# Nystromformer attention and a multiplicative FFN on one core: v pieces gated later, q landmarks' block form on GpSimd, the last chunk on two engines and two queues

## The chip, the cores and the metric

The kernel runs on one core of one Trainium2 chip. The time is device microseconds of one execution. A kernel's time is the median of its runs. A profile is one execution recorded by the hardware profiler; its span goes from the first to the last instruction, and times inside a trace count from the span's start.

## The reference

Attention by landmarks for 8 batches and 8 heads, 576 rows of 64, then a feed-forward network on all 4608 rows:

```python
q_lm = q.reshape(B, H, 32, 18, D).mean(axis=3)      # 32 landmarks, each the mean of 18 rows
k_lm = k.reshape(B, H, 32, 18, D).mean(axis=3)
A  = softmax(q    @ k_lm.T / 8)                     # 576 x 32
Bm = softmax(q_lm @ k_lm.T / 8)                     # 32 x 32
C  = softmax(q_lm @ k.T    / 8)                     # 32 x 576
Z  = Bm.T / (norm1(Bm) * norminf(Bm) + 1e-6)
for _ in range(6):
    Z = 2 * Z - Z @ Bm @ Z
x = (A @ Z @ C @ v)                                 # heads side by side: 4608 x 512
out = ((x @ w1) * (x @ w2)) @ w3 @ w_out            # widths 512, 1024, 1024, 512
```

All inputs and the output are float32.

## The kernel before

**Start and fold.** The kernel first multiplies w3 and w_out into one matrix `w34` (`fold`, lines 472 to 516; its matmuls are L497, its transposes L484), while q, k and v of the first batches arrive. The attention of batch 0 is woven into that by hand (lines 598 to 611).

**The loop over batches.** `for b in range(B)` (lines 616 to 643) has two halves. In the up half, for each of eight column groups j, `up(st, j, 0)` and `up(st, j, 1)` multiply batch b by the two up weights (L439, PSUM tiles `big`). ScalarE copies the first product to `a_sb` (L443), VectorE multiplies it with the second into `ab` (L445). In the down half `down` multiplies 128 rows at a time by `w34`, in two halves of four matmuls (L457); after the second half ScalarE copies the sums to `o_sb` (L461) and SyncE stores them (L467). An even batch has four such chunks, an odd one five; the last batch's fifth ends the program.

**What runs beside it.** Between these steps the loop advances a generator, `attention(sts[b + 1])`, by `steps(at)`: five steps in the up half, one behind it, the rest in the down half. Its first step (lines 199 to 213) adds the two landmark parts on TensorE (L201), copies them to fp16 `lm` on ScalarE (L206), and builds `qbd` (L208): the q landmarks laid out in blocks, where each pair of heads has its landmarks in the upper or the lower 64 partitions and zeros elsewhere, by a product with the 0/1 column pair `par`. The second step makes the 32 x 32 scores (L217, L221) and their softmax on VectorE (L224 to L230). The third and fourth make the scores of C (`scores_c`, L242, which read `qbd`), their exponentials `ect` (L246) and partial sums on GpSimd (L253 to L258). The fifth multiplies them with v (`cv`, L323 and L328). Six inversion steps (L382) and the product with the up weights (L425) follow.

**Loads.** For batch b + 2 the loop sends four DMA transposes of q and k on SyncE at the start of block b (`turn_all`, L106), four pieces of v in its up half (`load_v_piece`, L84 and L85), and at j = 5 the landmark sums on GpSimd (`landmarks`, L183 to L192), among which GpSimd issues the q and k loads of batch b + 3 (`qk_pieces`, L93). A v piece is 288 KB, two heads. ScalarE writes one column of its tile first (L84), and the DMA on SyncE waits for that write, so the place of the copy in ScalarE's queue holds the load back. In the version before, the copy reads `a_sb`, at j = 4, 5, 6 and 7.

**What sets the order.** Each engine runs its instructions in program order, which is written out by hand (`manual_schedule`). PSUM has three `big` tiles of two banks, one `small` and one `acc`; a tile is written again when its last reader is done, and which one a product gets is decided when the kernel is built. SyncE's queue holds transposes, v pieces and stores, GpSimd's holds its sums and the q and k loads.

Of the kernel before, what the change touches and what calls it, by code (L numbers as in the profile page):

```python
# [9 lines left out]
AXF = mybir.ActivationFunctionType  # L10
ALU = mybir.AluOpType
AX = mybir.AxisListType

B = 8
H = 8
S = 576
# [4 lines left out]
DM = 512  # L21
# [3 lines left out]
X64 = 64.0  # L25
NP = 96
# [5 lines left out]
def kernel(  # L32
# [11 lines left out]
    nc = tc.nc  # L44
# [8 lines left out]
    def big():  # L53
        return psp.tile([128, 2, 512], FP32, name="big", bufs=3)
# [25 lines left out]
    def load_v_piece(st, b, i, done):  # L80
        if i == 0:
            st["vt"] = pin.tile([128, H, 384], FP32, name="vt")
        hs = slice(2 * i, 2 * i + 2)
        nc.scalar.copy(out=st["vt"][0:NP, 2 * i, 0:1], in_=done)  # L84
        nc.sync.dma_start(out=st["vt"][0:NP, hs],  # L85
                          in_=v[b, hs].rearrange("h (p r) d -> p h (r d)", p=NP))

    def qk_pieces(st, b):
        st["qkn"] = pin.tile([128, 2, H, 384], FP16, name="qkn")
        for t, src in ((1, k), (0, q)):  # L90
            for i in range(2):
                hs = slice(4 * i, 4 * i + 4)
                nc.gpsimd.dma_start(out=st["qkn"][0:NP, t, hs, :],  # L93
                                    in_=src[b, hs].rearrange("h (p r) d -> p h (r d)", p=NP))
                yield
# [29 lines left out]
    ident = consts.tile([128, 128], FP32, name="ident")  # L125
# [49 lines left out]
    def landmarks(st, t, eng=nc.gpsimd, pieces=iter(())):  # L175
        if "parts" not in st:
            st["parts"] = pz.tile([128, 2, 2, H, 32], FP16, name="parts")
        for h0 in ((0,) if eng is nc.gpsimd else (0, 4)):
            own, n = ("", H) if eng is nc.gpsimd else ("v", 4)
            hs = slice(h0, h0 + n)  # L180
            x = st["qkT"][:, t, hs, :, :]
            tr = pat.tile([128, n, NP], FP32, name="tr" + own, bufs=1)
            eng.tensor_tensor(out=tr, in0=x[:, :, 0, :], in1=x[:, :, 1, :], op=ALU.add)  # L183
            eng.tensor_tensor(out=tr, in0=tr, in1=x[:, :, 2, :], op=ALU.add)  # L184
            next(pieces, None)
            t3 = tr.rearrange("p h (l g) -> p h l g", g=3)
            o = pat.tile([128, n, 32], FP32, name="o3" + own, bufs=1)
            hi, lo = st["parts"][:, 0, t, hs, :], st["parts"][:, 1, t, hs, :]
            eng.tensor_tensor(out=o, in0=t3[:, :, :, 0], in1=t3[:, :, :, 1], op=ALU.add)
            eng.tensor_tensor(out=o, in0=o, in1=t3[:, :, :, 2], op=ALU.add)  # L190
            eng.tensor_copy(out=hi, in_=o)
            eng.tensor_tensor(out=lo, in0=o, in1=hi, op=ALU.subtract)  # L192
            next(pieces, None)


    def attention(st, bank=None):
# [3 lines left out]
        for i in range(2):  # L200
# [4 lines left out]
        lm = pat.tile([128, 2, H, 32], FP16, name="lm")  # L205
        nc.scalar.copy(out=lm, in_=pl)  # L206
        qbd = pat.tile([128, H, 2, 32], FP16, name="qbd")
        nc.vector.tensor_tensor(  # L208
            out=qbd,
            in0=lm[:, 0, :, :].unsqueeze(2).to_broadcast([128, H, 2, 32]),  # L210
            in1=par.unsqueeze(1).unsqueeze(3).to_broadcast([128, H, 2, 32]),
# [3 lines left out]
        for qd in range(2):  # L215
            for h in range(4):
# [5 lines left out]
                             func=AXF.Exp, scale=SCALE / (GRP * GRP))  # L222
# [27 lines left out]
        def presum(qd):  # L250
# [21 lines left out]
                                scalar1=-1.0, scalar2=-1e-6, op0=ALU.mult, op1=ALU.add)  # L272
# [8 lines left out]
            out=bmbd, in0=bmn.unsqueeze(2).to_broadcast([128, 2, 4, 32]),  # L281
# [29 lines left out]
        for qd in range(2):  # L311
            nc.vector.tensor_scalar(out=sz_[:, qd, 0:32], in0=psR[:, 32 * qd:32 * qd + 32],
                                    scalar1=nrn[:, qd:qd + 1], scalar2=None, op0=ALU.mult)
            nc.vector.scalar_tensor_tensor(
                out=tz_[:, qd, :], in0=psR[:, 32 * qd:32 * qd + 32], scalar=nrn[:, qd:qd + 1],
# [58 lines left out]
        for it in range(6):  # L374
            last = it == 5
            psI = big()
            o = 32 if last else 0
# [25 lines left out]
        for qd in range(2):  # L403
# [7 lines left out]
                                       op0=ALU.mult, op1=ALU.subtract)  # L411
# [5 lines left out]
        for n in range(2):  # L417
            for w in range(2):
# [11 lines left out]
                else:  # L430
                    nc.vector.tensor_scalar(out=g[:, :, w, fs], in0=psG, scalar1=1.0 / ZS,  # L431
                                            scalar2=None, op0=ALU.mult)
            yield

    def up(st, j, w):
        p = big()
        for qd in range(2):
            for c in range(2):
                nc.tensor.matmul(p[:, c, 0:HS], st["g"][:, qd, w, 128 * j:128 * j + 128],  # L439
                                 st["ahat"][qd][:, c, :], start=(qd == 0), stop=(qd == 1))  # L440
        if w == 0:
            st["a_sb"] = po.tile([128, 2, HS], FP16, name="a_sb", bufs=2)
            nc.scalar.copy(out=st["a_sb"], in_=p[:, :, 0:HS])  # L443
        else:
            nc.vector.tensor_tensor(  # L445
                out=st["ab"][:, j, st["t0"]:st["t0"] + S].rearrange("p (c s) -> p c s", c=2),
                in0=st["a_sb"], in1=p[:, :, 0:HS], op=ALU.mult)


    rows = out.rearrange("(b p g) f -> b g p f", b=B, g=6)  # L450

    def down(ab, b0, t0, half, hold, bank):
        if half == 0:
            hold["ps"] = bank()
        pso = hold["ps"]
        for j in range(4 * half, 4 * half + 4):
            nc.tensor.matmul(pso[:, :], ab[:, j, t0:t0 + 128], w34[:, j, :],  # L457
                             start=(j == 0), stop=(j == 7))
        if half == 1:
            o_sb = po.tile([128, DM], FP32, name="o_sb")  # L460
            nc.scalar.activation(out=o_sb, in_=pso[:, :], func=AXF.Copy,  # L461
                                 scale=1.0 / (X64 * X64))
            o = 0
            while o < 128:
                gi, p0 = divmod((t0 + o) % S, NP)
                n = min(128 - o, NP - p0)
                nc.sync.dma_start(out=rows[b0 + (t0 + o) // S, 2 * (gi % 3) + gi // 3, p0:p0 + n, :],  # L467
                                  in_=o_sb[o:o + n, :])
                o += n


# [46 lines left out]
    sts = [dict() for _ in range(B)]  # L518

    def turn_all(b):  # L520
        for t in (1, 0):
            for h0 in (0, 4):
                transposes(sts[b], t, range(h0, h0 + 4))

    def steps(g, n=1):
        for _ in range(n):
            next(g, None)
# [3 lines left out]
    with tc.tile_pool(name="pf", bufs=2) as pf:  # L531
# [64 lines left out]
        turn_all(1)  # L596
        steps(fd, 6)
        at = attention(sts[0])
        for n, m in enumerate((2, 2, 2, 3, 3, 2, 1, 1, 1, 1, 2, 2, 3, 3)):
            steps(at)  # L600
# [10 lines left out]
        steps(fd, 64)  # L611
    pab = ctx.enter_context(tc.tile_pool(name="pab", bufs=2))
    at = attention(sts[1], acc)


    for b in range(B):
        st = sts[b]
        if b % 2 == 0:
            ab = pab.tile([128, 8, 2 * S], FP16, name="ab")
        st["ab"], st["t0"] = ab, S * (b % 2)  # L620
        if b + 2 < B:
            turn_all(b + 2)
        chunks = range(0, 512, 128) if b % 2 == 0 else range(512, 2 * S, 128)
        for j in range(8):
            up(st, j, 0)
            steps(at, (1, 1, 1, 0, 1, 0, 1, 0)[j])
            if b + 2 < B and j > 3:
                load_v_piece(sts[b + 2], b + 2, j - 4, st["a_sb"][0:NP, 0, 0:1])
            up(st, j, 1)
            if b + 2 < B and j == 5:  # L630
                pieces = qk_pieces(sts[b + 3], b + 3) if b + 3 < B else iter(())
                landmarks(sts[b + 2], 1, pieces=pieces)
                landmarks(sts[b + 2], 0, pieces=pieces)
        steps(at, 1)
        nxt = attention(sts[b + 2], acc) if b + 2 < B else iter(())
        hold = {}
        nd = 2 * len(chunks)
        for n in range(nd):
            bank = (lambda: big()[:, 0, :]) if n // 2 % 2 else acc
            down(ab, b - b % 2, chunks[n // 2], n % 2, hold, bank)  # L640
            steps(at)
        steps(at, 30)
        at = nxt
# [30 lines left out]
```

## Time and profile before

| | us |
|---|---|
| median of 4 runs | 289.15 |
| the runs | 285.31, 287.9, 290.39, 294.48 |
| profiled execution | 285.31 |
| its span | 283.5 |

The profile is of the fastest of these runs; about 1.8 us of its time lie around the span. TensorE is busy for 270.5 us of the span (95%), VectorE for 165.7, GpSimd for 153.2 and ScalarE for 130.2. In the page a group's row gives the line, the engine, the operation, output and input tiles with their shapes and the count, then busy time, the mean duration of one in ns, and the idle time of the engine just before these instructions with what ended it. The chain of work is followed back from the last instruction to what released each step; "issue" in it is time in which the engine waited for nothing that the profile shows. PEld is the weight load of TensorE, SPq and ACTq are the queues from which SyncE and ScalarE issue DMAs. The DMA engines are busy for nine tenths of most slices until 225 us and for less after that.

### The profile page before, as it was taken

How to read it: one execution, taken by the hardware profiler on the slowest of the kernel's cores; microseconds unless marked ns; L12 is line 12 of the kernel's file. 1: busy time of each engine (PE TensorE's matmuls, PEld its weight loads, DVE VectorE, ACT ScalarE, POOL GpSimd, SP SyncE). 2: the span in 40 equal slices, each digit the busy share in tenths (PEclk: the TensorE clock that was granted, in tenths of full speed). 3: DMA queues.
4: the chain of work that ended last, by engine and by line, in shares of the span. 5: the costliest groups of instructions: out<-in, count | busy, mean ns of one | idle time of the engine just before them, and what ended most of it. 6: DMA issues, size and time to landing. Idle time of an engine off the chain costs nothing.

```text
span 283.5 us, 9486 instructions
## 1 busy us (share of the span) xinstructions
PE 270.5 (95%) x3996; PEld 152.3 (54%) x3996; DVE 165.7 (58%) x430; ACT 130.2 (46%) x235; POOL 153.2 (54%) x202
## 2 busy tenths in 40 slices
PE   7999899999999997999999999998999999999993
PEld 3466455444674475347645754574458446834741
DVE  7743144653577575746766775576577756675620
ACT  2643254223661664157527732672276245625531
POOL 1617824595179739942895499259917950500000
PEclk9999999999999999999999999999999999999999
DMA  6999999999946999997898989997899622013024
GB/s 207 312 242 260 233 248 159 199 238 121 146 124 129 185 164 183 180 172 150 193 161 164 171 208 181 178 169 182 146 180 161 186 79 76 5 37 91 24 71 114
DMA packets 61978, 45.57 MB, mean 161 GB/s; under 512 B 35568, under 2 KB 54000, under 8 KB 61936
## 3 DMA queue, kind: packets, MB, share of 16 engines
q1 hardware_dynamic: 47392, 32.12, 49.5%
q0 software_dynamic: 13824, 11.54, 30.2%
q10 hardware_dynamic: 720, 1.31, 1.4%
q8 instruction: 31, 0.51, 0.8%
q14 instruction: 11, 0.09, 0.1%
HBM read 38.80 MB, written 9.44 MB: 170 GB/s over the span
## 4 chain that ended last, share of the span: by engine, by line
PE 83%; ACT 5%; POOL 4%; issue 3%; DVE 2%; DMA 1%; ACTq 0%; DVEq 0%; POOLq 0%
PE big L439 22%; PE acc L457 13%; PE big L457 11%; PE acc L497 10%; PE big L382 6%; PE big L425 5%; ACT a_sb L443 3%; PE small L323 2%; PE big L367 2%; PE acc L323 2%; PE big L484 2%; PE big L242 2%; DMA w3f<-in_moe_w_dram 1%; PE small L497 1%; PE big L292 1%
## 5 line engine op out<-in xcount | busy, mean ns | idle before, releaser
L439 PE MATMUL big<-ahat,gt 128*128 128x288 f16 x512 | 73.3, 286 | 2.0 <-ACT a_sb L443 1.6
L439 PEld LDWEIGHTS <-gt 128*128 128x128 f16 x512 | 48.4, 98 | 21.4 <-issue 7.4
L445 DVE TENSOR_TENSOR ab<-a_sb,big 128x576 f16<-128x576 f16 x64 | 48.0, 749 | 14.6 <-ACT a_sb L443 10.8
L443 ACT CAST a_sb<-big 128x576 f16<-128x576 f32 x64 | 40.9, 639 | 32.2 <-PE big L439 31.1
L253 POOL TENSOR_TENSOR t<-ect 96x384 f32<-96x384 f32 x16 | 15.9, 994 | 62.4 <-ACT ect L246 53.8
L497 PE MATMUL acc<-wsp,w3t 128*128 128x512 f16 x168 | 40.6, 379 | 0.7 <-ACT w L500 0.5
L457 PE MATMUL acc<-w,ab 128*128 128x512 f16 x160 | 40.3, 381 | 0.0
L457 PEld LDWEIGHTS <-ab 128*128 128x128 f16 x288 | 24.0, 98 | 29.0 <-issue 4.2
L457 PE MATMUL big<-w,ab 128*128 128x512 f16 x128 | 32.7, 381 | 0.0
L461 ACT ACTIVATE o_sb<-acc 128x512 f32<-128x512 f32 x20 | 11.9, 597 | 42.0 <-PE acc L457 42.0
L183 POOL TENSOR_TENSOR tr<-qkT 128x768 f32<-128x768 f16 x16 | 26.3, 1642 | 7.3 <-DMA qkT<-qkn 7.3
L497 PEld LDWEIGHTS <-w3t 128*128 128x128 f16 x192 | 18.1, 98 | 20.6 <-issue 1.8
L431 DVE TENSOR_SCALAR gt<-big 128x1024 f16<-128x1024 f32 x16 | 19.6, 1225 | 15.3 <-PE big L425 15.3
L184 POOL TENSOR_TENSOR tr<-tr,qkT 128x768 f32<-128x768 f32 x16 | 26.3, 1641 | 1.3
L429 ACT ACTIVATE gt<-big 128x1024 f16<-128x1024 f32 x16 | 16.4, 1024 | 11.9 <-PE big L425 11.9
L490 DVE SCALAR_TENSOR_TENSOR w3t<-big,w3t 128x512 f16<-128x512 f32 x16 | 11.0, 690 | 14.0 <-ACT w3t L489 14.0
L461 ACT ACTIVATE o_sb<-big 128x512 f32<-128x512 f32 x16 | 9.6, 597 | 19.0 <-PE big L457 19.0
L425 PE MATMUL big<-wup,zt 64*32 64x512 f16 x512 | 17.4, 380 | 0.7 <-issue 0.7
L489 ACT ACTIVATE w3t<-big 128x512 f16<-128x512 f32 x16 | 9.5, 594 | 12.4 <-PE big L484 12.3
L208 DVE TENSOR_TENSOR qbd<-lm,par 128x512 f16<-128x512 f16 x8 | 5.5, 692 | 15.8 <-ACT lm L206 15.8
L246 ACT ACTIVATE ect<-big 96x768 f32<-96x768 f32 x16 | 12.9, 807 | 3.6 <-PE big L242 2.9
L190 POOL TENSOR_TENSOR o<-o,tr 128x256 f32<-128x256 f32 x16 | 12.9, 806 | 1.3
(317 smaller groups left out, 373.1 us busy)
## 6 DMA issues: line engine op xcount, KB each, us to landing
vt<-in_v_dram SPq DMA_DIRECT2D x28, 288.0 KB, 4.5
out_dram<-o_sb SPq DMA_DIRECT2D x24, 192.0 KB, 3.2
qkn<-in_k_dram POOLq DMA_DIRECT2D x12, 288.0 KB, 5.3
qkn<-in_q_dram POOLq DMA_DIRECT2D x12, 288.0 KB, 5.5
w3f<-in_moe_w_dram SPq DMA_DIRECT2D x6, 512.0 KB, 7.0
out_dram<-o_sb SPq DMA_DIRECT2D x24, 128.0 KB, 3.4
wup<-in_moe_w_dram POOLq DMA_DIRECT2D x4, 512.0 KB, 32.2
out_dram<-o_sb SPq DMA_DIRECT2D x24, 64.0 KB, 2.9
```

What stands on the lines that cost most here:

```text
L183: eng.tensor_tensor(out=tr, in0=x[:, :, 0, :], in1=x[:, :, 1, :], op=ALU.add)
L184: eng.tensor_tensor(out=tr, in0=tr, in1=x[:, :, 2, :], op=ALU.add)
L382: nc.tensor.matmul(psI[32 * t:32 * t + 32, qd, o:96], tz_[sl, qd, :], sz_[sl, qd, o:96], start=True, stop=True, tile_position=(32 * h, 32 ...
L425: nc.tensor.matmul(psG[32 * h:32 * h + 32, qd, :], zt[rs, i, h, :], wup[rs, h, w, fs], start=(i == 0), stop=(i == 1), tile_position=(64 * ...
L429: nc.scalar.activation(out=g[:, :, w, fs], in_=psG, func=AXF.Copy, scale=1.0 / ZS)
L431: nc.vector.tensor_scalar(out=g[:, :, w, fs], in0=psG, scalar1=1.0 / ZS, scalar2=None, op0=ALU.mult)
L439: nc.tensor.matmul(p[:, c, 0:HS], st["g"][:, qd, w, 128 * j:128 * j + 128], st["ahat"][qd][:, c, :], start=(qd == 0), stop=(qd == 1))
L443: nc.scalar.copy(out=st["a_sb"], in_=p[:, :, 0:HS])
L445: nc.vector.tensor_tensor(out=st["ab"][:, j, st["t0"]:st["t0"] + S].rearrange("p (c s) -> p c s", c=2), in0=st["a_sb"], in1=p[:, :, 0:HS], ...
L457: nc.tensor.matmul(pso[:, :], ab[:, j, t0:t0 + 128], w34[:, j, :], start=(j == 0), stop=(j == 7))
L461: nc.scalar.activation(out=o_sb, in_=pso[:, :], func=AXF.Copy, scale=1.0 / (X64 * X64))
L497: nc.tensor.matmul(psW[j][:, :], turned[j, c // 4][:, a, c % 4, :], wsp[:, b, c, :], start=(c == 0 and a + b == 0), stop=(c == 7 and a == 1))
```

## The change

Three edits. The product that forms `qbd` is issued on GpSimd instead of VectorE. The four v pieces of batch b + 2 are issued at j = 6 and 7 and behind the first and the second finished chunk of the down half, and the column written ahead of each comes from the constant `ident` instead of `a_sb`. For the last chunk of the last batch (`final`), VectorE copies columns 256 to 511 and ScalarE columns 0 to 255 of the sums, and the second of its two stores (96 rows; the first has 32) goes out on ScalarE's DMA queue.

```diff
@@ -205,7 +205,7 @@ attention
         nc.scalar.copy(out=lm, in_=pl)
         qbd = pat.tile([128, H, 2, 32], FP16, name="qbd")
-        nc.vector.tensor_tensor(
+        nc.gpsimd.tensor_tensor(
             out=qbd,
             in0=lm[:, 0, :, :].unsqueeze(2).to_broadcast([128, H, 2, 32]),
             in1=par.unsqueeze(1).unsqueeze(3).to_broadcast([128, H, 2, 32]),
@@ -458,14 +458,20 @@ down
             o_sb = po.tile([128, DM], FP32, name="o_sb")
-            nc.scalar.activation(out=o_sb, in_=pso[:, :], func=AXF.Copy,
+            final = b0 == B - 2 and t0 == 2 * S - 128
+            if final:
+                nc.vector.tensor_scalar(out=o_sb[:, 256:DM], in0=pso[:, 256:DM],
+                                        scalar1=1.0 / (X64 * X64), scalar2=None, op0=ALU.mult)
+            c = slice(0, 256 if final else DM)
+            nc.scalar.activation(out=o_sb[:, c], in_=pso[:, c], func=AXF.Copy,
                                  scale=1.0 / (X64 * X64))
             o = 0
             while o < 128:
                 gi, p0 = divmod((t0 + o) % S, NP)
                 n = min(128 - o, NP - p0)
-                nc.sync.dma_start(out=rows[b0 + (t0 + o) // S, 2 * (gi % 3) + gi // 3, p0:p0 + n, :],
-                                  in_=o_sb[o:o + n, :])
+                eng = nc.scalar if final and o else nc.sync
+                eng.dma_start(out=rows[b0 + (t0 + o) // S, 2 * (gi % 3) + gi // 3, p0:p0 + n, :],
+                              in_=o_sb[o:o + n, :])
                 o += n
@@ -624,8 +630,8 @@ the loop over batches
         for j in range(8):
             up(st, j, 0)
             steps(at, (1, 1, 1, 0, 1, 0, 1, 0)[j])
-            if b + 2 < B and j > 3:
-                load_v_piece(sts[b + 2], b + 2, j - 4, st["a_sb"][0:NP, 0, 0:1])
+            if b + 2 < B and j > 5:
+                load_v_piece(sts[b + 2], b + 2, j - 6, ident[0:NP, 0:1])
             up(st, j, 1)
@@ -638,6 +644,8 @@
             down(ab, b - b % 2, chunks[n // 2], n % 2, hold, bank)
+            if b + 2 < B and n in (1, 3):
+                load_v_piece(sts[b + 2], b + 2, 2 + n // 2, ident[0:NP, 0:1])
             steps(at)
```

## The prediction

> **What bounds the kernel now.** I read the page first (engines, slices, chain by engine), then the chain of work in order of time for one block of the steady loop, then the timeline of that block by engine, then the waits and the tail. The page's engine line and its chain line say the same thing:
>
> ```profile
> PE 270.5 (95%) x3996; PEld 152.3 (54%) x3996; DVE 165.7 (58%) x430; ACT 130.2 (46%) x235; POOL 153.2 (54%) x202
> PE 83%; ACT 5%; POOL 4%; issue 3%; DVE 2%; DMA 1%; ACTq 0%; DVEq 0%; POOLq 0%
> ```
>
> TensorE sets the time; whatever the other engines do counts only where TensorE stands still for it. The granted clock is 0.998, so no clock effect is in these numbers. The batch blocks start (first L439 matmul) at 71.7, 97.55, 126.89, 153.03, 180.69, 207.67, 235.33 and 261.29. In a block the chain is matmul after matmul with one short break, at its start (block 3):
>
> ```profile
> 155.26 1.24 PE big L439 x8
> 156.50 0.03 ACTq L443
> 156.53 0.04 issue
> 156.57 0.65 ACT a_sb L443
> 157.21 0.04 issue
> 157.25 2.26 PE big L439 x16
> ```
>
> The page's "issue" share has a second break, in block 1 only, in the middle of a run of small matmuls:
>
> ```profile
> 109.10 0.04 PE acc L328 x5
> 109.14 1.50 issue
> 110.64 0.20 PE acc L328 x2
> ```
>
> and its table of DMA queues has the likely reason, TensorE's program arriving in 31 pieces of 16 KB:
>
> ```profile
> q8 instruction: 31, 0.51, 0.8%
> ```
>
> One piece starts at 108.09 and takes 1.10 us; matmuls resume 1.45 us after it. Block 4 has the same picture: a piece from 192.34 to 193.43, TensorE idle until 194.92, 1.49 us after it. The waits name DVE ab L445 for that (1.3 us at the longest, where the other six blocks have about 0.25), but the same instruction in block 3 started 0.06 us after the ab it needs. So 1.5 + 1.0 = 2.5 us are lost to late program pieces in the blocks.
>
> **qbd on GpSimd.** Per batch one VectorE instruction goes and one GpSimd instruction comes. The timeline of block 3:
>
> ```profile
> 154.27 0.59 ACT L206 CAST lm<-small 128x512 f16<-128x512 f32 x1
> 154.89 0.69 DVE L208 TENSOR_TENSOR qbd<-lm,par 128x512 f16<-128x512 f16 x1 [0.50 <-ACT lm L206]
> 155.50 0.75 DVE L445 TENSOR_TENSOR ab<-a_sb,big 128x576 f16<-128x576 f16 x1
> 156.32 0.69 PE L242 MATMUL big<-qbd,qkT 128*96 128x64 f16 x12
> 157.99 0.99 POOL L253 TENSOR_TENSOR t<-ect 96x384 f32<-96x384 f32 x1 [4.98 <-ACT ect L246]
> ```
>
> GpSimd is idle from 153.0 to 157.99, so it can start when lm is done, at 154.93. Its duration is not in the trace; the nearest row is the other product of broadcasts, L280:
>
> ```profile
> L280 POOL TENSOR_TENSOR bmbd<-bmn,mask 128x256 f32<-128x256 f32 x8 | 5.8, 730 | 0.6
> ```
>
> Against L277 (64 elements, 290 ns) that is 440/192 = 2.3 ns an element, so 512 elements take 730 + 256 x 2.3 = 1.32 us. The low end is the slope from L253 (384, 994) to L183 (768, 1642): 1.21; the high end is L190's 806/256 = 3.15 ns: 1.61. I take 1.32: qbd is ready at 156.25, where TensorE reaches L242 at 156.32. Nothing is lost. There is more cover: after L242's 12 matmuls (0.53 us of issue) TensorE waits for a_sb until 157.25 anyway, so qbd may come as late as 156.72, a duration of 1.73 us.
>
> What VectorE gains: the first ab no longer queues behind qbd. It needs the matmuls that end at 154.62, so it runs 154.7 to 155.45 instead of to 156.25. The L224 to L230 chain then waits only for ebm (155.91), 0.22 earlier, and so does the second ab (ends 157.6, not 157.82). The L439 group that takes the bank of this second ab started at 157.88, 0.63 after its forerunner at 157.25, where a free-running group takes 0.49; 0.13 us go. The stall before 157.25 stays: its a_sb waits for TensorE itself. So 7 x -0.13 = **-0.9 us** (if a different PSUM bank is handed out, the 0.15 before 155.84 may go as well: -2.0; with 1.73 us passed by 0.3: +2). In the fold, qbd ends at 37.3 where L242 starts at 38.87: nothing.
>
> The Trainium skill speaks against this edit: GPSIMD Engine Reference, "Engine selection", sends two-input elementwise work to VectorE, about 2x faster. Its factor of 1.96 on the 692 ns of L208 is 1.36 us, by which the edit would cost 8 x 0.67 = +5.4 us if it lay on the path. The row it has to be read with is L253's idle time, 4.98 us here and 53.8 in the page: the engine is empty there, and the sum by the trace is 0 or below. I go by the trace.
>
> **v pieces later.** In blocks 0 to 5 the four gates (0.19 us on ACT) and DMAs (288 KB on SP) move from j = 4, 5, 6, 7 to j = 6, 7 and to the first and second finished chunk. In block 3 the issues were at 162.0, 162.6, 164.2, 166.6; they become 164.2, 166.6, about 170.9 and 173.2 (each behind two stores of its chunk). The first was already late, as SP was sending transposes until 161.86. No gate waits for anything: the constant is always there and the vt buffer was read a block ago. On ACT two gates leave a stretch where it waits for TensorE anyway, and the new ones stand behind an o_sb copy, where ACT idles 2.0 to 2.5 us: zero. On SP, behind the last piece come stores (175.1) and, at 182.5, the next transposes: free. v is used in the next block, at 190.7, 17 us after its issue, for a landing of 4.5: hidden. In the DMA engines 576 KB now run beside the q and k pieces of GpSimd; at the 300 GB/s of the page's busiest slices (312 at most) that is an estimated 1.9 us. The last q piece (issued 152.32 in block 2, 5.5 to landing) would land at 159.7 instead of 157.8; the transpose that reads it goes out at 160.0, and GpSimd reads the result at 171.7. Hidden, with 7 us in reserve.
>
> What it can bring is the program pieces. In block 1 v issues at 107.1 and 108.6, just when the piece of 108.09 is wanted, and in block 4 at 189.4 and 190.3, before the one of 192.34. The Trainium skill, Runtime: NRT & Kernel Launch, "Instruction fetch mechanics", calls crossing a 16 KB boundary mostly hidden, because instructions go out slower than they arrive: by that rule this part is worth 0. The trace has 1.5 and 1.0 us, where TensorE runs through 256 instructions in 2.1 us (106.9 to 109.0). The transposes stay in the way, so I take a third of 2.5 us off, -0.8. Against it stands block 2: its piece landed at 140.08 and was needed at 141.82, 0.3 us more than the 1.45; a v piece now comes at 138. I put +0.4 on that. Sum **-0.4 us** (ends -2.5 and +1.5).
>
> **Last chunk.** Now:
>
> ```profile
> 277.23 1.74 PE acc L457 x8
> 279.04 0.60 ACT o_sb L461
> 279.66 0.32 SPq L467 DMA_DIRECT2D out_dram<-o_sb  x1
> 280.03 0.42 SPq L467 DMA_DIRECT2D out_dram<-o_sb  x1
> ```
>
> The second store's landing (2.3 us) ends the program: it is seen at 282.3, then 1.2 us of closing. Half the copy on ACT: 272 ns at 128 (L409), 597 at 512, so 380 at 256. On VectorE: 290 at 128 (L392), 1225 at 1024 (L431), so 420. Both end at 279.46, not 279.64: -0.18. The second store no longer waits 0.37 for the first to be issued: -0.37. Sum **-0.5 us** (ends -0.6, and +0.3 if the two copies run one after the other).
>
> **Sum.** -0.9 - 0.4 - 0.5 = -1.8 us. The profiled execution took 285.31 (span 283.5), so it would take 283.5. The runs shown lie between 285.31 and 294.48, median 289.15; the same 1.8 off the median is **287.3 us**. About 2% (5.8 us) is what a measurement of this kernel can tell from no change.
>
> **Rivals.**
> - *qbd outlasts its cover* (slower). Place: L242 at the start of each block, waiting for GpSimd. Up to 1.73 us it costs nothing; from there each 0.1 us costs 0.7 over seven blocks. At 2.6 us, twice my value: 7 x 0.87 = +6.1, less the tail and fetch gains: 294.4. For: no row has this mix of fp16, fp32 and two broadcasts. Against: all rows lie on 1.7 to 3.2 ns an element. Chance 0.13.
> - *Program pieces hit harder* (slower or level). v in the later stretches delays other pieces, block 2's above all: six blocks at +0.5 are +3.0; with -0.9 and -0.5 that makes +1.6: 290.8. For: those pieces took up to 1.95 us. Against: between chunks 256 instructions last some 7 us. Chance 0.12.
> - *All fetch stalls go, and banks fall well*: -2.5 - 2.0 - 0.5 = -5.0: 284.2. Chance 0.13.
> - *The edits do nothing measurable*, as each was hidden: 289.2. It lies within my own range; chance 0.1.
> The forecast keeps 0.52. The range runs from 283.0 (all gains, a quiet median) to 292.0 (pieces hit, or qbd at 2 us). Beyond 2% slower: half of the first rival and some scatter of the median, 0.15; faster: part of the third and scatter, 0.12; within: 0.73.
>
> **What would show it.** Right: L208 on POOL at about 1.3 us, L242 not waiting for it, the second ab 0.2 earlier, block 4 near 26.2 us instead of 26.98, L328's 1.50 smaller, the end 0.5 closer to the last matmul. Wrong: TensorE waiting for POOL qbd, new "issue" breaks in blocks 2 or 3, L183 waiting for qkT, or a v piece that L323 waits for.

## The result, and the profile after

The changed kernel took 282.79 us (median of 39 runs, 280.73 to 289.77), the kernel before 285.44 (median of 60). The ratio is 0.9914, with a 95% interval of 0.9894 to 0.9934: about 2.5 us faster, within the 2% called no change. The ratio leaves out runs more than 1.5% above the fastest of the same kernel. The four runs shown beforehand, with their median of 289.15, lay high: 3.7 us above the median of sixty. The forecast of 287.3 was 4.5 us too high.

The profiled execution of the changed kernel was one of its slower ones (285.04 us, span 283.3), so sums are made from other profiles too, above all from one of the same kernel in experiment twelve (282.17 us).

First the profile page of the kernel after. The three lines are the engines, the chain's shares and the row of the moved product (busy time and mean ns, then idle time ahead of it and what ended it):

```profile
PE 269.5 (95%) x3996; PEld 152.2 (54%) x3996; DVE 161.7 (57%) x423; ACT 128.9 (46%) x235; POOL 161.5 (57%) x210
...
PE 84%; POOL 4%; ACT 4%; issue 3%; DVE 1%; DMA 1%; ACTq 0%; DVEq 0%; POOLq 0%
...
L208 POOL TENSOR_TENSOR qbd<-lm,par 128x512 f16<-128x512 f16 x8 | 8.3, 1041 | 28.8 <-ACT lm L206 28.8
```

The eight products took 5.5 us on VectorE and take 8.3 on GpSimd, whose 28.8 idle us before them show that it was free. The bound is what it was, TensorE at 95%.

Now the start of block 3, which begins at 154.03. The chain of waits in order of time (start, length, what):

```profile
155.13 0.98 PE big L439 x8
156.11 0.15 PE acc L217 x8
156.26 1.10 PE big L439 x8
157.36 0.02 issue
157.38 0.65 ACT a_sb L443
158.03 0.04 issue
158.07 0.99 PE big L439 x6
```

The break before the next L439, with `a_sb` in it, has stayed, as TensorE itself releases that `a_sb`. That copy starts 3.35 us into the block (157.38 - 154.03), where before it was 3.54 (156.57 - 153.03): most of what was gained lies ahead of it. The timeline of the same stretch shows where:

```profile
155.27 0.59 ACT L206 CAST lm<-small 128x512 f16<-128x512 f32 x1
155.72 0.76 DVE L445 TENSOR_TENSOR ab<-a_sb,big 128x576 f16<-128x576 f16 x1 [0.33 <-PE big L439]
155.94 1.04 POOL L208 TENSOR_TENSOR qbd<-lm,par 128x512 f16<-128x512 f16 x1 [2.04 <-ACT lm L206]
157.18 0.69 PE L242 MATMUL big<-qbd,qkT 128*96 128x64 f16 x12
157.89 0.72 DVE L445 TENSOR_TENSOR ab<-a_sb,big 128x576 f16<-128x576 f16 x1
```

The first `ab` starts 1.69 us into the block instead of 2.47. `qbd` is ready at 156.98, and L242 starts at 157.18 without waiting. Counted from the block's start, the fourth to the seventh L439 group began at 2.16, 2.80, 4.22 and 4.85 before, and at 2.16, 2.66, 4.04 and 4.63 after. So 0.14 us goes at the fifth group, 0.04 more at the next and 0.04 at the one behind it, 0.22 in all. Two lines of the timeline before go with this:

```profile
155.15 0.64 ACT L443 CAST a_sb<-big 128x576 f16<-128x576 f32 x1 [0.28 <-PE big L439]
157.11 0.71 DVE L445 TENSOR_TENSOR ab<-a_sb,big 128x576 f16<-128x576 f16 x1
```

Before, the fifth group started at 155.83, 0.04 us after this copy to `a_sb` had ended (155.79) and so freed its `big` tile. After, the same copy ends 2.75 us into the block and the fifth group starts at 2.66 without it: it writes another tile, and the one free by then is that of the first `ab`, which ended at 2.45. The second `ab` ends 4.58 us into the block instead of 4.79, and the seventh group follows it.

The break in block 1 is still there, in the same run of L328 (chain of waits of the kernel after):

```profile
110.06 0.04 PE acc L328 x4
110.10 1.64 issue
111.74 0.23 PE acc L328 x3
```

The one in block 4 has shrunk. The timeline before, and the chain after:

```profile
194.92 0.40 PE L382 MATMUL big<-sz__3479,tz__3480 32*32 32x96 f32 x16 [1.00 <-DVE ab L445]
```

```profile
192.85 1.21 PE big L439 x9
194.06 0.30 issue
194.35 0.53 PE big L439 x3
```

At the end, in the timeline, the two copies stand one behind the other, and the trace names the first as what released the second:

```profile
278.49 0.42 DVE L463 TENSOR_SCALAR o_sb<-acc 128x256 f32<-128x256 f32 x1 [7.75 <-PE acc L457]
278.95 0.38 ACT L466 ACTIVATE o_sb<-acc 128x256 f32<-128x256 f32 x1 [1.60 <-DVE o_sb L463]
279.36 0.38 ACTq L473 DMA_DIRECT2D out_dram<-o_sb  x1
```

The block lengths, from one block's first L439 matmul to the next one's, put it together. They come from one profile each. Experiments six and two were profiled in the fastest of their 22 runs, so their breaks may be small ones.

| block | 0 | 1 | 2 | 3 | 4 | 5 | 6 | sum |
|---|---|---|---|---|---|---|---|---|
| before | 25.85 | 29.35 | 26.14 | 27.66 | 26.98 | 27.66 | 25.96 | 189.60 |
| after | 25.67 | 29.29 | 26.01 | 27.44 | 26.10 | 27.47 | 25.70 | 187.68 |
| e1, `qbd` alone | 25.67 | 28.67 | 25.81 | 28.15 | 26.68 | 27.45 | 25.69 | 188.12 |
| e2, v alone | 25.85 | 29.67 | 25.96 | 27.65 | 25.96 | 27.66 | 25.96 | 188.71 |
| e3, the tail alone | 25.85 | 29.39 | 26.13 | 27.66 | 27.04 | 28.35 | 25.96 | 190.38 |
| e4, both | 25.66 | 28.76 | 25.81 | 27.91 | 26.48 | 27.45 | 25.70 | 187.77 |
| e5, `qbd` made twice | 26.30 | 29.48 | 26.54 | 28.76 | 26.41 | 28.05 | 26.35 | 191.89 |
| e6, `qbd` later on VectorE | 25.76 | 29.29 | 26.06 | 27.49 | 25.74 | 27.49 | 25.74 | 187.57 |
| e7, no v loads | 25.67 | 28.93 | 25.70 | 27.44 | 25.98 | 27.44 | 25.69 | 186.85 |
| e8, no transposes | 25.67 | 28.33 | 25.88 | 27.44 | 25.69 | 27.44 | 25.70 | 186.15 |
| e11, v all in the down half | 25.66 | 30.54 | 26.01 | 27.44 | 25.75 | 27.45 | 25.69 | 188.54 |
| e12, the change again | 25.66 | 28.74 | 25.82 | 27.44 | 25.87 | 27.44 | 25.69 | 186.66 |

The start of the first block is not in the table: over all profiles it lies between 69.64 and 73.78 us. Without TensorE's idle time ahead of it, it lies between 68.3 and 69.3 in all of them. In the kernel after it came 1.36 us later than before (73.06 to 71.70), which with the tail's +0.28 eats most of the 1.92 that its blocks gained. Nearly all of that is two breaks of the same kind as in blocks 1 and 4: TensorE stood still for 0.98 us ahead of the L382 at 53.55 and for 1.21 ahead of the L425 at 63.55, each some 1.4 to 1.5 us after a program piece had landed. Before, the same two were 0.24 and 0.67.

### The profile page after: what moved, and what is told of

The parts are those of the page before. It is cut to its first block, busy times and chain, and to the rows that moved or that the text cites. A ratio compares the mean times of both kernels' runs of the same rounds, so it can differ in the third digit from the quotient of the medians.

```text
span 283.3 us, 9504 instructions
## 1 busy us (share of the span) xinstructions
PE 269.5 (95%) x3996; PEld 152.2 (54%) x3996; DVE 161.7 (57%) x423; ACT 128.9 (46%) x235; POOL 161.5 (57%) x210
## 4 chain that ended last, share of the span: by engine, by line
PE 84%; POOL 4%; ACT 4%; issue 3%; DVE 1%; DMA 1%; ACTq 0%; DVEq 0%; POOLq 0%
PE big L439 22%; PE acc L457 13%; PE big L457 11%; PE acc L503 10%; PE big L382 6%; PE big L425 5%; ACT a_sb L443 2%; PE small L323 2%; PE big L367 2%; PE small L503 2%; PE acc L323 2%; PE big L242 2%; PE big L490 2%; PE big L292 1%; DMA w3f<-in_moe_w_dram 1%
## 5 line engine op out<-in xcount | busy, mean ns | idle before, releaser
L439 PE MATMUL big<-ahat,gt 128*128 128x288 f16 x512 | 72.2, 286 | 2.0 <-ACT a_sb L443 1.4
L439 PEld LDWEIGHTS <-gt 128*128 128x128 f16 x512 | 48.4, 98 | 20.3 <-issue 5.5
L466 ACT ACTIVATE o_sb<-acc 128x512 f32<-128x512 f32 (+1 forms) x20 | 11.7, 587 | 42.3 <-PE acc L457 40.7
L431 DVE TENSOR_SCALAR gt<-big 128x1024 f16<-128x1024 f32 x16 | 19.6, 1225 | 15.9 <-PE big L425 15.9
L208 POOL TENSOR_TENSOR qbd<-lm,par 128x512 f16<-128x512 f16 x8 | 8.3, 1041 | 28.8 <-ACT lm L206 28.8
L429 ACT ACTIVATE gt<-big 128x1024 f16<-128x1024 f32 x16 | 16.4, 1024 | 11.9 <-PE big L425 11.9
L425 PE MATMUL big<-wup,zt 64*32 64x512 f16 x512 | 17.4, 380 | 1.2 <-issue 1.2
```

Of the source, the lines that this page charges most:

```text
L425: nc.tensor.matmul(psG[32 * h:32 * h + 32, qd, :], zt[rs, i, h, :], wup[rs, h, w, fs], start=(i == 0), stop=(i == 1), tile_position=(64 * ...
L429: nc.scalar.activation(out=g[:, :, w, fs], in_=psG, func=AXF.Copy, scale=1.0 / ZS)
L466: nc.scalar.activation(out=o_sb[:, c], in_=pso[:, c], func=AXF.Copy, scale=1.0 / (X64 * X64))
```

## Theory and rivals

**The theory:** the three edits act apart. `qbd` leaves VectorE's queue, the first two `ab` run earlier, and two PSUM tiles come free earlier, in each of seven blocks. The v pieces leave the DMA engines to the program piece of block 4. The two copies of the last chunk run in turn, so that edit costs a little. **The rivals:** the gain is VectorE's or GpSimd's load and not the place in the queue; the late program pieces have another cause than v; the tail's cost comes from the second queue. Experiments 1 to 3 do one edit each, 4 joins the first two, and the rest takes single suspects apart. e1 to e3 start from the kernel before, e5 to e11 from e4.

## The experiments

**e1: the first edit alone.**

```diff
-        nc.vector.tensor_tensor(
+        nc.gpsimd.tensor_tensor(
             out=qbd,
```

> The kernel before with the qbd product on GpSimd and nothing else. Theory A (the gain is VectorE's queue: the first ab no longer stands behind qbd, and another PSUM bank comes free first): blocks 0 to 6 each 0.20 to 0.26 us shorter where no program piece is late, L439 groups 5 and 6 of a block at 2.65 and 4.03 us instead of 2.80 and 4.21; in all -1.6 us, ratio 0.994. Rival B (the gain comes from the v pieces): the L439 groups may move, but the time stays within 0.3 us, ratio 0.999 or more.

Measured: 283.2 us, ratio 0.9923 (0.9890 to 0.9956). The L439 groups of block 3 start at 2.66, 4.04 and 4.63 as in the full change, so the 0.22 us a block is this edit's. Blocks 5 and 6, with no broken stretch, are 0.21 and 0.27 shorter. Block 4 keeps its break:

```profile
189.93 1.21 PE big L439 x9
191.13 0.89 issue
192.02 0.53 PE big L439 x3
```

Block 3 is 0.7 us longer than the 27.44 of the full change (28.15), with a break at one L425, 1.2 us after a program piece landed. e4 (27.91) and e5 have a longer block 3 too, the full change in neither profile; why is open.

**e2: the second edit alone.**

```diff
-            if b + 2 < B and j > 3:
-                load_v_piece(sts[b + 2], b + 2, j - 4, st["a_sb"][0:NP, 0, 0:1])
+            if b + 2 < B and j > 5:
+                load_v_piece(sts[b + 2], b + 2, j - 6, ident[0:NP, 0:1])
...
+            if b + 2 < B and n in (1, 3):
+                load_v_piece(sts[b + 2], b + 2, 2 + n // 2, ident[0:NP, 0:1])
```

> The kernel before with the v pieces at j = 6, 7 and behind chunks 0 and 1, and nothing else. Theory A (v takes part in late program pieces only): the block starts of the L439 groups stay at 2.80 and 4.21 us; block 4's stall at L382 shrinks from 1.0 us extra to about 0.3, block 1's stays at 1.5 or more; -0.5 to -1.0 us, ratio 0.997. Rival B (v is the main gain): -1.8 us or more, ratio 0.994 or less.

Measured: ratio 0.9965 (0.9931 to 0.9998), about 1.0 us. The medians of all runs, 285.41 and 285.52, hardly differ. In the chain, block 4 runs through without a break:

```profile
190.42 1.58 PE big L439 x12
192.00 0.34 PE big L382 x16
```

while block 1 has a longer one than before:

```profile
107.04 0.04 PE acc L328 x5
107.08 1.83 issue
108.91 0.20 PE acc L328 x2
```

So the edit moves what it was expected to move in block 4, and does not help block 1.

**e3: the third edit alone** (the diff of the tail as in the change).

> The kernel before with the last chunk's two copies and two queues, and nothing else. Theory A (the two copies run one after the other): VectorE's copy 0.42 us, then ScalarE's 0.38, stores issued 0.25 us later after the last matmul than before, the end 0.1 to 0.3 us later; ratio 1.000 to 1.001. Rival B (the after profile was an exception and the two queues gain): the end 0.3 to 0.5 us earlier, ratio 0.998 to 0.999.

Measured: ratio 1.000 (0.9969 to 1.003). Counted from the start of the last matmul, VectorE's copy begins at 0.475, ScalarE's at 0.933, the stores are issued at 1.342 and 1.347, and the program ends at 5.23. Before, the one copy begins at 0.47, the stores go out at 1.09 and 1.46, and the end is at 4.96. The edit costs 0.26 us, which is within the interval of the timed ratio; the trace tells it.

**e4: the first two edits, without the third.**

> The change without its last edit: qbd on GpSimd and the later v pieces, the last chunk as before. If the last edit costs (theory A), this is 0.2 to 0.3 us faster than the changed kernel: -2.7 us, ratio 0.9905, and its time from the last matmul to the end is 4.6 us as before. If the last edit gains (rival B), it is 0.3 to 0.5 us slower than the changed kernel: ratio 0.993.

Measured: 281.97 us, ratio 0.9873 (0.9824 to 0.9921), and the end 4.96 after the start of the last matmul, as before. The two edits add: 0.9923 x 0.9965 is 0.9888. Leaving the tail edit out loses nothing.

Each run lists the mean clock that TensorE was granted, and it differs from run to run (e11 shows why that matters). In the runs of e1 to e4 and of the kernel before beside them that were granted 0.996 or more, the medians are 284.36 before (29 runs), 282.84 for e1 (14), 283.44 for e2 (9), 284.89 for e3 (14) and 281.97 for e4 (6). That is -1.5, -0.9, +0.5 and -2.4 us, close to what the traces give for each edit.

**e5: the product made twice on GpSimd.**

```diff
+        nc.gpsimd.tensor_tensor(
+            out=qbd,
+            in0=lm[:, 0, :, :].unsqueeze(2).to_broadcast([128, H, 2, 32]),
+            in1=par.unsqueeze(1).unsqueeze(3).to_broadcast([128, H, 2, 32]),
+            op=ALU.mult)
```

> qbd on GpSimd and the later v pieces, last chunk as before, and the qbd product issued twice in a row on GpSimd (2 x 1.04 us). Theory A (GpSimd's time is covered up to a point): with one product L242 has slack; lm ends 1.83 us into a block, so qbd would come at 1.9 + 2.08 = 4.0, where L242 could start at 3.14 and its successor at 4.03. Blocks get 0.4 to 0.6 us longer, 3.5 us in all, ratio near 1.000. Rival B (GpSimd is never on the path, there is always room): blocks unchanged, ratio 0.987.

Measured: ratio 1.0049 (1.0014 to 1.0083). The added lines shift the numbers, so L242 is L247 here. The timeline of block 3:

```profile
158.02 1.04 POOL L208 TENSOR_TENSOR qbd<-lm,par 128x512 f16<-128x512 f16 x1 [1.92 <-ACT lm L206]
159.14 1.04 POOL L213 TENSOR_TENSOR qbd<-lm,par 128x512 f16<-128x512 f16 x1
160.23 0.68 PE L247 MATMUL big<-qbd,qkT 128*96 128x64 f16 x12 [0.80 <-POOL qbd L213]
```

With the product at 158.02 to 160.18, 2.16 us, the scores wait 0.80 for it, and the blocks grow by 0.6 (blocks 0, 5 and 6 against e4). So it has about 1.5 us (2.16 less the 0.6 that a block grows) before it costs anything, and needs 1.04. Of the slower rival the place and the price are real; the duration that it needed was not.

**e6: the product back on VectorE, but behind the first `ab`.**

```diff
+        yield
-        nc.gpsimd.tensor_tensor(
+        nc.vector.tensor_tensor(
             out=qbd,
...
-        yield
```

> qbd back on VectorE, but issued at the start of the attention's second step, behind the first ab; later v pieces, last chunk as before. Theory A (what counts is that the first ab does not stand behind qbd, so that its bank comes free first): group 5 at 2.65 us as with GpSimd; but L224 to L230 and the second ab now stand behind qbd and are 0.2 us later than with GpSimd, so a block is 0.1 to 0.2 us longer than there; ratio 0.989 to 0.992. Rival B (VectorE needs the 0.69 us themselves): blocks as before the change, ratio 0.997.

Measured: ratio 0.9952 (0.9923 to 0.9980). The timeline of block 3:

```profile
152.85 0.76 DVE L445 TENSOR_TENSOR ab<-a_sb,big 128x576 f16<-128x576 f16 x1 [0.33 <-PE big L439]
153.53 0.68 DVE L209 TENSOR_TENSOR qbd<-lm,par 128x512 f16<-128x512 f16 x1
154.36 0.70 PE L242 MATMUL big<-qbd,qkT 128*96 128x64 f16 x12
155.20 2.15 PE L439 MATMUL big<-ahat,gt 128*128 128x288 f16 x15
```

The groups start at 2.66, 4.04 and 4.68: nearly those of GpSimd, and the blocks without a break are 0.05 longer (27.49 and 25.74, against 27.44 and 25.69; block 0 is 0.10 longer than e4's). So by the trace the gain comes from letting the first `ab` pass, not from the engine that makes `qbd`. The timed ratio came out above what was expected for this, and its interval also holds the 0.9965 of the late v alone: the time by itself does not show the gain. At a granted clock of 0.996 or more the median is 283.53 us (12 runs) against 284.85 before (23), -1.3 us, where 0.05 x 7 = 0.35 us off e4's -2.4 would be about -2.0. Whether something in the rest of the program costs more is open.

**e7: no v loads in the loop.**

```diff
-            if b + 2 < B and j > 5:
-                load_v_piece(sts[b + 2], b + 2, j - 6, ident[0:NP, 0:1])
+            if b + 2 < B and j == 6:
+                sts[b + 2]["vt"] = st["vt"]
...
-            if b + 2 < B and n in (1, 3):
-                load_v_piece(sts[b + 2], b + 2, 2 + n // 2, ident[0:NP, 0:1])
```

> qbd on GpSimd, last chunk as before, and no v loads in the loop over batches: batches 2 to 7 use the v of batch b - 2, which leaves out 6.75 MB of loads. Theory A (v traffic delays program pieces): the stalls of blocks 1 and 4 (1.3 and 1.0 us with the later v) both fall below 0.7; 0.5 to 1.5 us faster than with the later v. Rival B (the transposes alone delay the pieces, or nothing does and TensorE simply outruns its supply): both stalls stay within 0.2 us.

This kernel leaves out 24 loads: batches 2 to 7 use the v of two batches before. Measured: ratio 0.9904 (0.9874 to 0.9933). TensorE stands still for 1.27 us in block 1, 1.39 us after a program piece landed, and for 0.18 in block 4. So v is not needed to make block 1's piece late, and with late v there is little left to gain in block 4 from v.

**e8: no transposes in the loop.**

```diff
-            turn_all(b + 2)
+            sts[b + 2]["qkT"] = st["qkT"]
```

> qbd on GpSimd and the later v pieces, last chunk as before, and no DMA transposes in the loop: batches 2 to 7 use the transposed q and k of batch b - 2, which leaves out 24 of the 28 transposes. Theory A (the transposes' packets, of 256 bytes, delay the program pieces most): the stalls of blocks 1 and 4 shrink to 0.5 us or less. Rival B (TensorE outruns its supply whatever the DMA load): block 1 keeps 1 us or more.

This kernel leaves out 24 transposes: batches 2 to 7 use the transposed q and k of two batches before. Measured: ratio 0.9874 (0.9810 to 0.9937), from four runs. Block 4 has no break, and block 1's is the shortest of all profiles (chain of waits):

```profile
108.54 0.05 PE acc L328 x5
108.59 0.66 issue
109.25 0.22 PE acc L328 x2
```

The change has 1.09 there in e12 and 1.64 in the profile shown above, and e9, with the transposes, 0.86. So 0.66 us stay when the transposes are gone. Whether they are part of the rest is not shown: it is one profile, and the kernels that keep them spread more widely than this step.

**e9: one copy as before, but the second store on ScalarE's queue.**

```diff
-                nc.sync.dma_start(
+                eng = nc.scalar if o and b0 == B - 2 and t0 == 2 * S - 128 else nc.sync
+                eng.dma_start(
```

> qbd on GpSimd, the later v pieces, the last chunk copied by ScalarE alone as before, only its second store on ScalarE's queue. Theory A (the copies in turn cost 0.25 us, the second queue by itself gains little because the store then lands later): both stores issued 1.09 us after the last matmul starts, the second 0.37 earlier than with one queue, its landing 2.3 to 2.6 us later; the tail 0.0 to 0.3 us shorter than with one queue, ratio 0.986 to 0.987. Rival B (two queues cost something of their own): the tail 0.1 us or more longer.

Measured: ratio 0.9876 (0.9834 to 0.9918). Its timeline shows the copy and the second store:

```profile
274.94 0.60 ACT L461 ACTIVATE o_sb<-acc 128x512 f32<-128x512 f32 x1 [1.13 <-PE acc L457]
275.56 0.38 ACTq L468 DMA_DIRECT2D out_dram<-o_sb  x1
```

Both stores go out within 0.01 us of each other, 1.09 us after the last matmul's start. The last one lands 2.59 us after that; from one queue it was 2.27 us after the second issue. So the last landing is 0.05 us earlier (3.68 against 3.73), and the end is at 4.98 against 4.96: nearly all of the 0.37 us of earlier issue is lost in the landing.

**e10: the last chunk as two halves of 256 columns**, each with eight matmuls into its own PSUM tile, its own copy on ScalarE and its own two stores, the second on ScalarE's queue, so that the first half is copied while the second is computed.

```diff
+    def last_chunk(ab, b0, t0):
+        for c in range(2):
+            cs = slice(256 * c, 256 * c + 256)
+            ps = small() if c else acc()
...
+            o_h = po.tile([128, 256], FP32, name="o_h", bufs=2)
+            nc.scalar.activation(out=o_h, in_=ps[:, 0:256], func=AXF.Copy, scale=1.0 / (X64 * X64))
```

> qbd on GpSimd, the later v pieces, and the last chunk in two column halves in two PSUM tiles: eight matmuls of 256 columns each, the first half copied and stored while the second is multiplied. Theory A (the copies ran in turn because they read one PSUM tile): only one copy of 0.38 us stands behind the last matmul, so its stores are issued 0.2 us earlier than with one whole copy and the second of them 0.4 more by the second queue; the matmuls take 0.1 us more; end 0.3 to 0.6 us earlier, ratio 0.985 to 0.986. Rival B (eight narrow matmuls are bound by their weight loads): the last chunk's matmuls take 0.5 us more and eat that up.

Measured: 281.73 us, ratio 0.9838 (0.9794 to 0.9882). The timeline of the end (the first copy lies beside the second half's matmuls):

```profile
273.41 1.04 PE L457 MATMUL acc<-w,ab 128*128 128x256 f16 x8
274.28 1.04 PE L457 MATMUL small<-w,ab 128*128 128x256 f16 x8
274.48 0.39 ACT L460 ACTIVATE o_h<-acc 128x256 f32<-128x256 f32 x1 [0.23 <-PE acc L457]
275.36 0.38 ACT L460 ACTIVATE o_h<-small 128x256 f32<-128x256 f32 x1 [0.49 <-PE small L457]
275.77 0.34 ACTq L466 DMA_DIRECT2D out_dram<-o_h  x1
```

From the last L439 matmul the sixteen narrow matmuls take 0.13 us more than the eight wide ones; the end comes 4.38 us after the last one's start. Net, that is 0.46 us less than one whole copy and 0.73 less than the change (13.04 us from the last L439 matmul to the end, against 13.50 and 13.77).

**e11: all four v pieces in the down half**, at n = 1, 3, 5 and 7, none at j = 6 and 7.

```diff
-            if b + 2 < B and j > 5:
-                load_v_piece(sts[b + 2], b + 2, j - 6, ident[0:NP, 0:1])
...
-            if b + 2 < B and n in (1, 3):
-                load_v_piece(sts[b + 2], b + 2, 2 + n // 2, ident[0:NP, 0:1])
+            if b + 2 < B and n in (1, 3, 5, 7):
+                load_v_piece(sts[b + 2], b + 2, n // 2, ident[0:NP, 0:1])
```

> qbd on GpSimd, last chunk as before, all four v pieces behind the chunks of the down half (none at j = 6 and 7). Theory A (v next to the dense matmuls of step five delays program pieces): block 1's stall at L328 below 1.2 us and block 4's at most 0.5, as in the kernel without v loads; ratio 0.985 to 0.987. Rival B (the q and k loads of the down half now come late): transposes wait for q on SyncE's queue, GpSimd waits for qkT, blocks 0.3 us or more longer; ratio 0.989 or more.

Measured: 284.33 us, ratio 0.9919 (0.9885 to 0.9954), above the intervals of e10 and e12 beside it. The ratio is what the rival expected, but not for its reason: blocks 2 to 6 are much as in e12, so no load of q or k became late. Block 1 took 30.54 us. TensorE stood still for 1.45 us at the program piece (1.09 in e12), and then twelve L439 matmuls took 2.67 us in the chain, where e12 has 1.58. The first line is e11, the second e12:

```profile
111.14 2.67 PE big L439 x12
109.56 1.58 PE big L439 x12
```

That second delay is the clock. From 111.4 to 114.9 us this profile shows a granted TensorE clock of 0.50; no other profile has such a stretch in its blocks. What brought it about is not shown: the longer break in e2 (1.83 us at the same place) left the clock at 1.00. One such stretch takes 0.006 off the mean clock of a run (3.4 x 0.5 / 283), and seven of the twelve runs lie below 0.996 (two of six in e12, none of six in e10). At 0.996 or more the median is still 283.47 us (5 runs) against 282.17 for e12 (4); what else is slower is open.

**e12: the changed kernel once more**, measured beside e9 to e11.

> The changed kernel itself beside the other three on one chip. Theory A (its last edit costs): 0.2 to 0.4 us slower than the same kernel with the old last chunk, tail 4.86 us against 4.59; ratio 0.988 to 0.992. Rival B (the tail of its first profile was an exception): tail 4.5 us or less.

Measured: 282.21 us, ratio 0.9840 (0.9809 to 0.9871). The two medians of the change lie 0.6 us apart, those of the kernel before 1.3 (285.44 and 286.71), and the two ratios of the same pair have intervals that do not meet. So ratios that were not measured side by side are not to be compared to better than about 0.7%. The intervals of e9, e10 and e12 overlap; that e10's tail is the best of them is told by its trace alone.

## Why the prediction was right or wrong

**What failed, in short.** The forecast of 287.3 us took -1.8 us off a median of four runs that lay 3.7 us high; that step made the number miss. In the -1.8 itself two terms were too small: `qbd`, as the wait for a PSUM tile at the fifth L439 group was held to stay, and v, as the 0.4 set against it for block 2 did not come. A third had the wrong sign, as the two copies were held to run together.

**The bound** was read rightly: TensorE, with only its own breaks worth anything.

**`qbd` on GpSimd: right mechanism, size too small.** The forecast was -0.13 a block and -0.9 us. Blocks without a break lost 0.18 to 0.27, about 0.22, which makes -1.6 over seven. Two terms were off. The product took 1.04 us; 1.32 was taken, from the slope of the fp32 products of L277 and L280, and even the low end of 1.21 was above it. That cost nothing in the sum, since it is hidden either way. The failed term is the PSUM tile: the sum took the 0.15 at the fifth L439 group as staying, and gave it to the end "if a different PSUM bank is handed out". It went, by 0.14, as the group starts show. The second `ab` ended 0.21 us earlier, as the forecast had it (0.22). The group behind it was to gain 0.13 of that, because its forerunner was to stay where it was; the forerunner moved by 0.18, and the group gained 0.22. The cover was put at 1.73 us (the forecast's own times, 154.93 to 156.72, give 1.79) and is about 1.5 (e5).

The Trainium skill's rule (GPSIMD Engine Reference, "Engine selection") of about 2x for VectorE is 1041 to 692 ns here, a factor of 1.50. As the forecast said, it does not decide: the product lies in GpSimd's idle time. But the rule's advice has something in it after all. e6 keeps the product on VectorE, 0.68 us long, and gets all but 0.05 us of the block's gain by issuing it one instruction later. The prediction named the place in the queue as the gain, but did not see that VectorE could have it too.

**v later: right mechanism in one block of two.** The forecast was -0.4 us: a third of the 2.5 us of late pieces, less 0.4 for block 2. e2 measured a ratio of 0.9965, -1.0 us, and in its trace block 4 alone is 1.02 us shorter. TensorE's idle time there is 0.89 to 1.07 us in the three profiles with v as before (before, e1, e3) and at most 0.30 in those with the late v but one (0.69 in e4). Block 1's is 1.50 before, 1.01 and 1.54 in e1 and e3, and between 0.86 and 1.83 with the late v (0.66 in e8, without the transposes): no change that can be told. There the step "v issues just when the piece is wanted" took a coincidence for a cause: without any v the gap is 1.27 (e7). The +0.4 for block 2 was not seen either; it is 26.14 before and 25.81 to 26.01 with both edits. The reading of the break itself fits all profiles: a piece lands 1.2 to 1.6 us before TensorE goes on (once 2.4, in block 1 of the kernel after), and in block 1 the gap is in the same run of L328 each time. It is argued and not shown, as no experiment moved a piece by itself; for block 4 before, the waits name `ab` instead. The forecast also looked for such breaks in the blocks alone. Two more are in the start, and in the profile after they cost 1.28 us more than before. The skill's "Instruction fetch mechanics" (Runtime: NRT & Kernel Launch), which calls that crossing mostly hidden, fits most other pieces, where TensorE shows no break, and not the 0.66 to 1.83 us in block 1, where TensorE runs through 256 instructions in 2.1 us.

**The tail: wrong.** The forecast was -0.5 us and it is +0.26, the sum's own other end, "if the two copies run one after the other". Two steps failed. That the halves run together: they do not, in any of three profiles with this edit, and 0.42 + 0.38 is longer than 0.60. That the second store's 0.37 comes off: e9 has it issued earlier and gains nothing at the end, as it lands later. Both copies read one PSUM tile, of 512 fp32 columns. Here the Trainium skill has a rule that the prediction passed over: PSUM — Partial Sum Buffer, "PSUM bank collisions raise a hardware error", says that two engines may not access one bank in the same 32 partitions at once, reads against reads included, and that the compiler puts a dependency between any two such instructions, even on different addresses. By that rule the sum is +0.3, by the prediction's rows -0.5. The trace agrees with the rule: ScalarE's copy is released by VectorE's and begins within 0.04 us of its end. The two copies also share the tile that they write, which would be another reason. Against it stand L429 and L431, here in the profile after: they write two parts of one `gt` too, but read two different `big` tiles, and overlap by 0.58 us.

```profile
153.72 1.02 ACT L429 ACTIVATE gt<-big 128x1024 f16<-128x1024 f32 x1
154.16 1.23 DVE L431 TENSOR_SCALAR gt<-big 128x1024 f16<-128x1024 f32 x1 [0.74 <-PE big L425]
```

No run splits the last chunk over two engines and two tiles; e10 has two tiles, but one engine.

**The sum and its base.** Measured apart, the edits give -1.6 - 1.0 + 0.26 = -2.3 us; the ratio 0.9914 is -2.5 of 285.44. The forecast was -1.8, by one term too small, one too small and one of the wrong sign. What made the number miss is the last step: putting that -1.8 on the median of four runs. The profiled execution, 285.31, was within 0.13 us of the median of sixty, and the sum against it, 283.5, is 0.7 us off. The range began at 283.0, reckoned from a high median, and so missed 282.79 by 0.2. That the profiled execution lay so near the median of sixty is luck: the one after, 285.04, lies 2.25 above its own.

Part of the scatter is the clock, which the forecast set aside because its one profile showed 0.998. Of the 55 runs of the kernel before beside e1 to e4, 29 were granted 0.996 or more and have a median of 284.36 us, 20 between 0.990 and 0.995 with 286.45, and 5 between 0.984 and 0.989 with 289.85. The clocks of three of the four first runs are not on record. Of the changed kernel's 40 listed runs 12 lie below 0.996, of the kernel before 63 of 123 beside the experiments. Even at 0.996 or more its median is 284.36, 284.85 or 286.01 us, depending on when it was measured, so the clock is not all. Whether the change makes such stretches rarer, and gains by that, is not shown.

**The rivals.** `qbd` outlasting its cover was refuted by its 1.04 us, and e5 shows where it would have begun. Pieces hitting harder did not happen in the blocks of the change; in e11 the break at the piece was no longer than before, and the clock did the rest. Of the case of all gains one part came, the PSUM tile; of the 2.5 us of fetch stalls about 1.0 went, and of the tail nothing.

**A version with a better end.** e10 is the change's first two edits with a tail that works, 281.73 us. Its trace ends 0.73 us nearer to the last L439 matmul than the change's. Its timed advantage over the change (0.9838 against 0.9840) is far inside their intervals.

## What to carry to other kernels

A short instruction that stands ahead of the one that frees a PSUM tile is worth moving, but ask first for its place in the queue and only then for its engine. Splitting the last copy over two engines pays only if both can run at once: if they read one PSUM tile, the trace shows the second waiting for the first. Let the first half be copied while the second is computed into another tile. Where the runs are few, forecast the change and not the time: the median of four was 3.7 us from the median of sixty, and one profiled execution 2.25 us from the median of its kernel, each about as much as the change or more. Look at the granted clock of each run before comparing times.

## What the runs showed of the hardware that had not been expected

- Two engines reading two halves of one PSUM tile ran in turn, 0.42 + 0.38 us, in all three profiles with that edit.
- Of two stores issued at once on two queues the last landed after 2.59 us (e9); issued 0.37 us apart on one queue, the second landed after 2.27. The time of the last landing hardly moved (3.68 and 3.73 us after the last matmul's start).
- In every profile TensorE stands still in the same run of short matmuls in block 1, for 0.66 to 1.83 us, and goes on 1.2 to 1.6 us after a 16 KB program piece has landed, once 2.4. Such breaks in the start of the program (up to 1.4 us, at L382 and L425) account for about half of the spread of its length.
- The granted TensorE clock can fall to one half for 3.4 us in the middle of a program that keeps TensorE busy for 95% of its span (e11, from 111.4 us): twelve L439 matmuls took 2.67 us there instead of 1.58.
- GpSimd's product of two broadcasts with 512 elements in fp16 took 1.04 us, 2.0 ns an element, where rows of the same engine in fp32 had pointed to 1.2 to 1.6.
